# Windowed attention and an MLP mixer on one core: the first pair's tail in one piece, seven-product units in batches 3 and 5, a new order of loads

## Chip, cores and metric

The kernel runs on one core of a Trainium2 chip. The metric is the device time of one execution in microseconds (us). Every number here is from the runs of the kernel before the change or from one profiled execution of it.

## What is computed

Eight batches of 576 positions, eight heads of 64. Attention looks back over a window of 128 positions with a linear bias for each head; its output, eight heads side by side, is the 512-wide input of a mixer with a layer over positions and a layer over channels.

```python
def _attn_ref(q, k, v):                       # each 8 x 8 x 576 x 64
    scores = scale * np.matmul(q, k.transpose(0, 1, 3, 2))
    bias = slopes[:, None, None] * (-np.abs(rel))[None, :, :]
    mask = (rel >= 0) & (rel < 128)
    scores = np.where(mask, scores + bias[None], -1e9)
    attn = np.exp(scores - np.max(scores, axis=-1, keepdims=True))
    attn = attn / (np.sum(attn, axis=-1, keepdims=True) + 1e-09)
    return np.matmul(attn, v)

def _moe_ref(x, w_tok1, w_tok2, w_ch1, w_ch2):  # x: 8 x 576 x 512
    xt = x.transpose(0, 2, 1)
    h = np.maximum(xt @ w_tok1, 0.0) @ w_tok2    # 576 -> 256 -> 576
    u = x + h.transpose(0, 2, 1)
    h2 = np.maximum(u @ w_ch1, 0.0) @ w_ch2      # 512 -> 1536 -> 512
    return u + h2
```

## The kernel before

**Tiles.** Batches go in pairs. A pair has nine blocks of 128 rows: blocks 0 to 3 are the first 512 positions of its first batch, 4 to 7 those of its second, and block 8 (`TAIL`) holds the last 64 positions of both, 64 rows each. Inputs are cast to bf16 as they are loaded, by DMAs that POOL issues (line 521). Five buffers hold q and k of a block, five hold v.

**Stages of a batch.** `side(b)` (line 887) is attention and the token layer: for each block its turn (q and k transposed into `qkT`), scores (line 684), exponential on ACT (line 707), mask on DVE (line 717), the product with v (line 750), reciprocal and scaling on DVE (lines 763 and 766). Then `token_mix`: the first token product (lines 795 and 805), its relu (line 813), the second (line 838), the addition that makes `ub` on DVE (line 856), and the turn of `ub` to `uT`, by TensorE for batches 0 and 1 and by DMA from SP after that (line 864). `main(b)` (line 1007) is the channel layer: `chunk(t)` computes one of twelve tiles of the hidden layer with four matmuls of 512 columns (line 1035) and a relu (line 1041); `tail_piece` does the tail (line 1078) in odd batches; then `second(b)` (line 1149) runs the second layer as seven products in place of eight (line 1212), which need sums of hidden tiles made on DVE (line 1060), and evicts them (line 1183). The order of the seven is the list `PRODUCTS`. `side(b + 1)` runs interleaved with `main(b)`.

**Turns.** A block is turned either by eight TensorE transposes (line 644) and a copy out of PSUM (line 650, on DVE or ACT), or by one DMA transpose from SP (line 633). `FROM_QK` is the running number of the first block that goes by DMA; the first pair has numbers 0 to 8.

**The first pair's tail.** Its q, k and v are loaded in two halves, one batch each. The first half is in the list `LOADS` as q8, k8, v8; the second half comes as lq8, lk8, lv8, later in the list, into the same buffer (`rewrites`). Two memsets (lines 542 and 543) clear the buffer's second half first. The block is turned in `side(0)` and again in `side(1)`, when the second half is there (the condition in line 900).

**Seven-product units.** `unit(b, u, ...)` (line 927) computes four hidden tiles at once by the same scheme of seven products in place of eight: 28 matmuls of 256 columns (line 957) for the 16 of 512 columns that four chunks have. Three of the seven products go one after the other over one PSUM bank after a first one, with the bank read in between. It needs four differences of `uT` made on DVE (`halves`, line 921), sums of weights made once (line 600), three copies out of PSUM (line 972), three additions (line 981), three relus in SBUF (line 983) and one relu out of PSUM (line 1001). `UNITS[b]` says how many of the three groups of four tiles of batch b go this way: before, three in batch 7 and none elsewhere. Units are the last groups of their batch.

**Order.** A planner in the kernel file (`Plan.run`, line 127) simulates the engines and puts the instructions of each engine in an order: of what is ready first, by rank. Ranks get random shifts from `SEEDS`, one per batch. `marks["wait"]` (line 1262) lists operations of `main(b)` that come only behind the last scores of `side(b + 1)`: with `UNIT_LATE` the first products of a unit, with `SECOND_LATE` those of the second layer. POOL's order is not planned: it is the order of `LOADS`, then the other pairs' blocks, then late stores. Where TensorE is idle early on, matmuls on zeros are put in (line 1268). `HALF`, `RATES` and the like are the planner's own figures; they only shape the order.

Of the kernel before, what the change touches and what calls it, by code (L numbers as in the profile page):

```python
# [20 lines left out]
class Buf:  # L21
    def __init__(self, ring, choice):
        self.ring, self.choice, self.slot = ring, choice, None
        self.writers, self.parts, self.users, self.later = [], {}, [], []
# [41 lines left out]
class Plan:  # L66
# [9 lines left out]
    def op(self, eng, cost, emit, rank, makes=(), adds=(), rewrites=(), part=None, uses=(), reads=(), needs=(),  # L76
# [4 lines left out]
        o = Op()  # L81
# [14 lines left out]
        for b in many(rewrites):  # L96
            o.deps.update(u for u in b.users if u not in b.later)
            b.later.append(o)
            b.writers.append(o)
            o.bufs.append(b)  # L100
        if part is not None:
            b, key = part
# [14 lines left out]
    def slot(self):  # L117
        self.orders += 1
        return self.orders

    def dma(self, emit, descs, packets, makes=(), rewrites=(), order=None, uses=()):
        o = self.op("POOL", 550 + 0.33 * descs, emit, 0, makes=makes, rewrites=rewrites, uses=uses,
                    order=order or self.slot())
        o.packets = packets
        return o
# [184 lines left out]
    def emit(self, spin):  # L310
# [12 lines left out]
        for _, _, go in sorted(work, key=lambda w: w[:2]):  # L323
# [8 lines left out]
FROM_QK = 10  # L332
# [8 lines left out]
PRODUCTS = [1, 5, 6, 2, 3, 7, 4]  # L341
# [5 lines left out]
SEEDS = [63488, 544433, 0, 603260, 673561, 0, 172207, 0, 0]  # L347
SHIFT = 1500.0
UNIT_LATE = True
SECOND_LATE = False  # L350
BIASED = [0, 1, 2]
THIRD = [(4, 5)]
TURNED = False
# [4 lines left out]
UNITS = [0, 0, 0, 0, 0, 0, 0, 3]  # L358
# [7 lines left out]
HALF = 0.7  # L366
# [3 lines left out]
LOADS = ("q2 k1 q1 v1 k2 k3 v0 q3 v2 v8 W1 q8 k8 v3 W2 k6 k5 q5 k4 q6 A0 q4 "  # L370
         "v4 lk8 lq8 k7 A1 q7 v5 A2 B0 v6 A3 v7 lv8 B1 B2 T0 P0 B3")
# [3 lines left out]
def kernel(  # L375
# [16 lines left out]
    P = nc.NUM_PARTITIONS  # L392
# [8 lines left out]
    TAIL = 2 * NC  # L401
# [109 lines left out]
    def load(name, pr, blk, parts, order=None):  # L511
        got = block(pr, blk)
        buf = got["v" if name == "v" else "qk"]
        src = {"q": q, "k": k, "v": v}[name]

        def to():
            return buf()[:, :, 0:D] if name == "v" else buf()[:, "qk".index(name), :, :]

        for b, s0, n, p0 in parts:
            def go(b=b, s0=s0, n=n, p0=p0):  # L520
                nc.gpsimd.dma_start(out=to()[p0 : p0 + n, :, :], in_=rows(src, b, s0, n))  # L521
            kw = {"makes": buf} if order is None else {"rewrites": buf, "order": order}
            plan.dma(go, n * H, 1024 if n == P else 520, **kw)
# [20 lines left out]
    lw1, lw2, lw2t, lc1, lc2, later = [], [], [], [], [], []  # L544
# [342 lines left out]
    def side(b, rank):  # L887
# [360 lines left out]
    for name, order in later:  # L1248
        load(name, 0, TAIL, parts_of(0, TAIL)[1:2], order)
# [52 lines left out]
```

## Time and profile before

| | |
|---|---|
| three runs | 280.22 us median (279.9 to 280.82) |
| profiled execution | 280.18 us; span from first to last instruction 278.0 us |
| granted TensorE clock | 1.000 (mean) |
| TensorE matmuls | busy 270.4 us, 97%, of it 8.9 us on zeros, all before 24.8 us |
| VectorE (DVE) | busy 210.0 us, 76% |
| ScalarE (ACT) | 136.2 us, 49% |
| GpSimd (POOL) | 116.3 us, 42%, issuing loads |

The span is 2.2 us shorter than the execution's time. Busy times of TensorE count a matmul to its modelled end, so neighbours overlap: sixteen matmuls of 512 columns show 379 ns each, yet follow each other at 216 ns. A matmul's price is therefore read from the start of one group to the start of the next.

### The profile page before, as it was taken

Reading aid. Unit: us, or ns where it says so; the run is one execution under the profiler, and the core shown is the slowest. Engines: PE = TensorE matmul, PEld = TensorE weight load, DVE = VectorE, ACT = ScalarE, POOL = GpSimd, SP = SyncE. Lnnn points to the kernel's source line nnn. Section 1 sums busy time; section 2 is a strip of 40 time slices with the busy share of each in tenths; the row PEclk is TensorE's granted clock in tenths of the full one; section 3 lists DMA queues with packets and bytes.
Section 4 is the critical chain, followed back from the end, with each engine's and each line's share of the span. In section 5 each row is a group of like instructions: output and inputs, shape, how many; then the busy total and the mean of one; then the engine's idle time right before and its main releaser. Section 6 shows DMA issues by size and latency. Waiting matters only on the chain.

```text
span 278.0 us, 7069 instructions
## 1 busy us (share of the span) xinstructions
PE 270.4 (97%) x2871; PEld 181.7 (65%) x2871; DVE 210.0 (76%) x486; ACT 136.2 (49%) x216; POOL 116.3 (42%) x146
## 2 busy tenths in 40 slices
PE   7989999999999999999999999999999999999994
PEld 4865755676686546595667655586666755489983
DVE  8467799968897569964898469862978569877972
ACT  5563996336970298007860087206951077215500
POOL 8998848940382018900594008800480320022000
PEclk9999999999999999999999999999999999999999
DMA  9999999999599689999999999979799930052014
GB/s 132 151 159 170 191 191 179 156 140 232 73 127 154 137 211 128 132 136 202 174 137 158 201 174 75 146 123 207 136 135 112 171 134 2 8 142 98 2 59 130
DMA packets 167535, 38.43 MB, mean 138 GB/s; under 512 B 155792, under 2 KB 166672, under 8 KB 167504
## 3 DMA queue, kind: packets, MB, share of 16 engines
q0 software_dynamic: 116112, 20.03, 92.5%
q1 hardware_dynamic: 50352, 17.70, 31.6%
q8 instruction: 22, 0.36, 0.5%
q10 hardware_dynamic: 1040, 0.26, 0.4%
q14 instruction: 9, 0.07, 0.1%
HBM read 35.85 MB, written 9.44 MB: 163 GB/s over the span
## 4 chain that ended last, share of the span: by engine, by line
PE 85%; DVE 6%; POOL 4%; DMA 2%; issue 0%; ACT 0%; POOLq 0%
PE ps L1212 25%; PE ps L1035 24%; PE ps L750 6%; PE ps L684 6%; PE ps L838 4%; PE ps L795 4%; PE ps L1078 4%; PE ps L1123 4%; PE ps L957 3%; POOL qk L521 2%; DMA v<-in_v_dram 2%; DVE s L1060 1%; POOL v L521 1%; PE ps L644 1%; DVE WT L582 1%; PE ps L873 1%
## 5 line engine op out<-in xcount | busy, mean ns | idle before, releaser
L1035 PE MATMUL ps<-uT,WC 128*128 128x512 bf16 x328 | 79.5, 379 | 0.0
L1041 ACT ACTIVATE r<-ps 128x512 bf16<-128x512 f32 x75 | 44.3, 602 | 57.4 <-PE ps L1035 52.9
L707 ACT ACTIVATE pe<-ps 128x1024 bf16<-128x1024 f32 (+1 forms) x76 | 63.5, 888 | 18.1 <-PE ps L684 17.7
L521 POOL DMA_DIRECT2D v<-in_v_dram x40 | 34.4, 862 | 89.9 <-PE ps L750 88.2
L1035 PEld LDWEIGHTS <-WC 128*128 128x128 bf16 x328 | 29.1, 98 | 28.3
L717 DVE TENSOR_TENSOR pe<-pe,mask 128x1024 bf16<-128x1024 bf16 (+1 forms) x62 | 37.1, 607 | 8.0 <-ACT pe L707 7.3
L1212 PEld LDWEIGHTS <-r 128*128 128x128 bf16 x384 | 36.9, 98 | 7.9 <-issue 0.7
L521 POOL DMA_DIRECT2D qk<-in_q_dram x39 | 34.0, 877 | 2.8 <-PE ps L750 1.4
L521 POOL DMA_DIRECT2D qk<-in_k_dram x39 | 34.1, 883 | 2.1 <-DMA v<-in_v_dram 1.1
L1212 PEld LDWEIGHTS <-s 128*128 128x128 bf16 x288 | 27.5, 98 | 6.3 <-issue 1.8
L766 DVE TENSOR_TENSOR xb<-ps,rt 128x256 bf16<-128x256 f32 (+1 forms) x73 | 29.5, 419 | 0.8
L750 PEld LDWEIGHTS <-pe 128*128 128x128 bf16 (+1 forms) x560 | 21.6, 100 | 9.6 <-DVE pe L717 2.6
L750 PE MATMUL ps<-v,pe 128*128 128x65 bf16 (+1 forms) x560 | 26.2, 194 | 1.2 <-DMA v<-in_v_dram 1.2
L1212 PE MATMUL ps<-WC,r 128*128 128x256 bf16 x192 | 25.4, 273 | 0.0
L1212 PE MATMUL ps<-WT,s 128*128 128x256 bf16 x192 | 24.2, 273 | 0.0
L1212 PE MATMUL ps<-WT,r 128*128 128x256 bf16 x192 | 23.7, 273 | 0.0
L1183 DVE TENSOR_TENSOR ob<-ps,ub 128x512 f32<-128x512 f32 x22 | 15.2, 689 | 10.1 <-PE ps L1212 10.0
L856 DVE TENSOR_TENSOR ub<-ps,xb 128x512 bf16<-128x512 f32 x34 | 21.4, 684 | 1.4 <-PE ps L838 1.2
L684 PEld LDWEIGHTS <-qkT 64*128 64x128 bf16 x560 | 14.8, 94 | 10.9 <-issue 9.7
L763 DVE RECIPROCAL rt<-ps 128x4 f32<-128x4 f32 (+1 forms) x76 | 12.3, 175 | 10.1 <-PE ps L750 9.4
L684 PE MATMUL ps<-qkT 64*128 64x128 bf16 (+1 forms) x304 | 19.4, 216 | 0.0
L838 PE MATMUL ps<-r,W 128*128 128x512 bf16 x64 | 16.1, 379 | 0.1
(96 smaller groups left out, 336.4 us busy)
## 6 DMA issues: line engine op xcount, KB each, us to landing
out_dram<-ob SPq DMA_DIRECT2D x17, 256.0 KB, 2.5
v<-in_v_dram POOLq DMA_DIRECT2D x32, 128.0 KB, 4.8
qk<-in_q_dram POOLq DMA_DIRECT2D x31, 128.0 KB, 4.9
qk<-in_k_dram POOLq DMA_DIRECT2D x31, 128.0 KB, 4.8
WC<-in_moe_w_ch_dram POOLq DMA_DIRECT2D x8, 384.0 KB, 9.0
out_dram<-raw SPq DMA_DIRECT2D x7, 256.0 KB, 2.6
out_dram<-ob POOLq DMA_DIRECT2D x5, 256.0 KB, 2.9
out_dram<-raw POOLq DMA_DIRECT2D x3, 256.0 KB, 3.0
```

The costliest lines, as they stand in the source:

```text
L521: nc.gpsimd.dma_start(out=to()[p0 : p0 + n, :, :], in_=rows(src, b, s0, n))
L684: pe_.matmul(wide(e)[:, i, kind, a:z], lhsT=ts[kb]()[e * D : (e + 1) * D, NHP + i, :], rhs=ts[blk]()[e * D : (e + 1) * D, i, a:z], start=n ...
L707: act_.activation(out=pb()[:, e, :, lo:, c0:c1_], in_=wide(e)[:, :, lo:, c0:c1_], func=ACT.Exp, scale=scale)
L717: dve_.tensor_tensor(out=o, in0=o, in1=heads(mk, es), op=ALU.mult)
L750: pe_.matmul(view()[a:z, at, i, :], lhsT=pb()[:, e, i, kind, a:z], rhs=vb()[:, h, 0 : D + 1], start=m == 0, stop=m == len(mms) - 1, skip_g ...
L766: dve_.tensor_tensor(out=x4(), in0=view()[r0:r1_, :, :, 0:D], in1=rt()[r0:r1_, 0:n, :, :].broadcast_to([r1_ - r0, n, 4, D]), op=ALU.mult)
L838: pe_.matmul(ht()[:, hs], lhsT=W2[:, j, c * P : (c + 1) * P], rhs=r1()[:, j, :], start=j == 0, stop=j == NJ - 1 and not fold)
L856: plan.op("DVE", 690, lambda blk=blk, ht=ht, hs=hs: dve_.tensor_tensor(out=ub()[:, blk, :], in0=ht()[:, hs], in1=xb()[:, blk, :], op=ALU.a ...
L1035: pe_.matmul(ct()[:, :], lhsT=WC1[:, cb, t * P : (t + 1) * P], rhs=uT()[:, cb, :], start=cb == 0, stop=cb == NCB - 1)
L1041: plan.op("ACT", 600, lambda t=t, ct=ct: act_.activation(out=r2()[:, t, :], in_=ct()[:, :], func=ACT.Relu), rk, part=(r2, t), uses=[ct], o ...
L1183: dve_.tensor_tensor(out=v, in0=bk().rearrange("p (c n) -> p c n", c=2), in1=src, op=ALU.add)
L1212: pe_.matmul(bk()[:, c * HN : (c + 1) * HN], lhsT=l(t, c), rhs=w(t), start=first, stop=g == 1 and t == HK - 1, skip_group_check=True)
```

## The change

The first pair's tail is loaded with both halves at its place in `LOADS` (still two DMAs for each of q, k and v), the memsets and the machinery for a later rewrite go, and it is turned once. `FROM_QK` goes from 10 to 9, so the first block of the second pair is turned by DMA. `UNITS` gives batches 3 and 5 one unit each. `SECOND_LATE` and `TURNED` are switched on: the second layer's opening products come behind the next side's last scores, and the bias matmuls of the first blocks (line 693) behind that block's turn. `PRODUCTS`, `SEEDS`, `LOADS` and `HALF` get other values.

```diff
 class Buf:
-        self.writers, self.parts, self.users, self.later = [], {}, [], []
+        self.writers, self.parts, self.users = [], {}, []
...
-    def op(self, eng, cost, emit, rank, makes=(), adds=(), rewrites=(), part=None, uses=(), reads=(), needs=(),
+    def op(self, eng, cost, emit, rank, makes=(), adds=(), part=None, uses=(), reads=(), needs=(),
            after=0.0, order=None, bus=0.0, other=None, mode=0, behind=()):
...
-        for b in many(rewrites):
-            o.deps.update(u for u in b.users if u not in b.later)
-            b.later.append(o)
-            b.writers.append(o)
-            o.bufs.append(b)
...
-    def slot(self):
+    def dma(self, emit, descs, packets, makes=(), uses=()):
         self.orders += 1
-        return self.orders
-
-    def dma(self, emit, descs, packets, makes=(), rewrites=(), order=None, uses=()):
-        o = self.op("POOL", 550 + 0.33 * descs, emit, 0, makes=makes, rewrites=rewrites, uses=uses,
-                    order=order or self.slot())
+        o = self.op("POOL", 550 + 0.33 * descs, emit, 0, makes=makes, uses=uses, order=self.orders)
...
-FROM_QK = 10
+FROM_QK = 9
...
-PRODUCTS = [1, 5, 6, 2, 3, 7, 4]
+PRODUCTS = [1, 5, 6, 2, 7, 3, 4]
...
-SEEDS = [63488, 544433, 0, 603260, 673561, 0, 172207, 0, 0]
+SEEDS = [299663, 80952, 553840, 849187, 0, 759155, 0, 0, 0, 0]
...
-SECOND_LATE = False
+SECOND_LATE = True
...
-TURNED = False
+TURNED = True
...
-UNITS = [0, 0, 0, 0, 0, 0, 0, 3]
+UNITS = [0, 0, 0, 1, 0, 1, 0, 3]
...
-HALF = 0.7
+HALF = 0.9
...
-LOADS = ("q2 k1 q1 v1 k2 k3 v0 q3 v2 v8 W1 q8 k8 v3 W2 k6 k5 q5 k4 q6 A0 q4 "
-         "v4 lk8 lq8 k7 A1 q7 v5 A2 B0 v6 A3 v7 lv8 B1 B2 T0 P0 B3")
+LOADS = ("k1 q1 k2 q3 k3 q2 v0 v3 W1 v1 q8 v2 k8 q5 v8 W2 k4 k5 k6 q4 A0 v5 "
+         "q6 q7 A1 v4 v6 k7 A2 A3 B0 v7 B1 B2 P0 T0 B3")
...
-    def load(name, pr, blk, parts, order=None):
+    def load(name, pr, blk, parts):
...
-            kw = {"makes": buf} if order is None else {"rewrites": buf, "order": order}
-            plan.dma(go, n * H, 1024 if n == P else 520, **kw)
+            plan.dma(go, n * H, 1024 if n == P else 520, makes=buf)
...
-    last = block(0, TAIL)
-    plan.op("DVE", 180, lambda b=last["qk"]: dve_.memset(b()[R:P, :, :, :], 0.0), -90, makes=last["qk"])
-    plan.op("DVE", 180, lambda b=last["v"]: dve_.memset(b()[R:P, :, 0:D], 0.0), -90, makes=last["v"])
...
-            load(what, 0, n, parts_of(0, n)[0:1])
-        elif what in ("lq", "lk", "lv"):
-            later.append((what[1], plan.slot()))
+            load(what, 0, n, parts_of(0, n))
...
-                    if (pr, w) not in qkT or (u == TAIL and pr == 0):
+                    if (pr, w) not in qkT:
                         transposes(pr, w, rank(0 if by_transfer(pr, w) else 450))
...
-    for name, order in later:
-        load(name, 0, TAIL, parts_of(0, TAIL)[1:2], order)
```

In `LOADS`, W1 and W2 are the token layer's weights, A0 to A3 quarters of the first channel layer's, B0 to B3 of the second's, P0 and T0 the small pieces of the token weights for the tail. W1 is two DMAs. Block 0's q and k come ahead of the list from SP and ACT (line 484).

More of the change, by code (lines that the diff above doesn't have):

```diff
@@ L346 @@
 SUMS_AT = 60e3
-SEEDS = [63488, 544433, 0, 603260, 673561, 0, 172207, 0, 0]
+SEEDS = [299663, 80952, 553840, 849187, 0, 759155, 0, 0, 0]
 SHIFT = 1500.0
 UNIT_LATE = True
-SECOND_LATE = False
+SECOND_LATE = True
 BIASED = [0, 1, 2]
 THIRD = [(4, 5)]
-TURNED = False
+TURNED = True
 SLANT = 4.0e3
@@ L540 @@
             plan.op("DVE", 190, lambda i=i: dve_.memset(W1p[(1 - i) * R : (2 - i) * R, i, :], 0.0), -90)
-    last = block(0, TAIL)
-    plan.op("DVE", 180, lambda b=last["qk"]: dve_.memset(b()[R:P, :, :, :], 0.0), -90, makes=last["qk"])
-    plan.op("DVE", 180, lambda b=last["v"]: dve_.memset(b()[R:P, :, 0:D], 0.0), -90, makes=last["v"])
-    lw1, lw2, lw2t, lc1, lc2, later = [], [], [], [], [], []
+    lw1, lw2, lw2t, lc1, lc2 = [], [], [], [], []
     for item in LOADS.split():
```

## Prediction

> **What bounds the kernel.** First the busy shares, then the 40 slices, then busy time by stage, last the chain.
>
> ```profile
> span 278.0 us, 7069 instructions
> PE 270.4 (97%) x2871; PEld 181.7 (65%) x2871; DVE 210.0 (76%) x486; ACT 136.2 (49%) x216; POOL 116.3 (42%) x146
> PE   7989999999999999999999999999999999999994
> ```
>
> TensorE (PE) is busy from the fourth slice on. Matmul ends are modelled, so I count idle time and pace instead: waits for other engines put down to PE total 3.2 us, of it 3.0 before 19 us (1.2 at the start, 0.6 on block 0's casts, 1.2 on v), and fillers on zeros end at 24.8 us. Before that point the loads decide, behind it whatever TensorE has to do.
>
> ```profile
> 18.81 0.40 PE L750 MATMUL ps<-v,pe 128*128 128x65 bf16 x8 [1.18 <-DMA v<-in_v_dram]
> 19.67 0.20 PE L684 MATMUL ps<-qkT 64*128 64x64 bf16 x2
> ...
> 23.37 0.59 PE L805 MATMUL ps<-xb,W1p 64*128 64x512 bf16 x2
> ...
> 24.63 1.03 PE L838 MATMUL ps<-r,W 128*128 128x512 bf16 x4
> ```
>
> In these lines of the timeline block 3's v lands at 18.8, the tail's scores follow at 19.7, and the last token product (L805) waits for the tail; L838 at 24.6 opens the dense part. Next, who has room there (busy us of PE, PEld, DVE, ACT, POOL in each stretch):
>
> ```profile
> 30.00:44.00 14.00, 14.00 (x196) 8.66 (x194) 12.74 (x39) 13.25 (x21) 9.60 (x13) 1.00 1.55 193
> 44.00:58.00 14.00, 13.83 (x117) 8.59 (x114) 13.63 (x28) 6.51 (x14) 11.86 (x16) 1.00 2.19 155
> 140.00:160.00 20.00, 20.00 (x202) 14.23 (x196) 14.56 (x30) 4.10 (x7) 8.99 (x11) 1.00 1.73 169
> 200.00:210.00 10.00, 10.00 (x141) 6.53 (x136) 7.80 (x22) 6.75 (x10) 7.50 (x9) 1.00 1.87 135
> ```
>
> From 30 to 58 DVE is nearly full as well, and ACT to 44; around 140 and 200, where batches 3 and 5 end their first layer, DVE has a quarter free. The chain agrees:
>
> ```profile
> PE 85%; DVE 6%; POOL 4%; DMA 2%; issue 0%; ACT 0%; POOLq 0%
> ```
>
> **Step 1, the tail turned once.** Eight transposes and a copy go. From the start at 33.85 to the next group's start at 34.30 eight cost 0.45 us. The copy was ACT's, 1.05 at 35.41, in the stretch where ACT is 13.25 of 14.00 busy. Credit 0.45; bounds 0, if DVE's full stretch behind it sets the pace anyway, and 0.45, since TensorE saves no more. The memsets at 4.4 (0.48 and 0.27) open block 0's casts; block 1 waits for its loads behind them, so no credit.
>
> **Step 2, block 0 of the second pair by DMA.** Eight transposes at 56.03 go (next start 56.48: 0.45), with ACT's 1.01 copy at 56.7, which nobody waited for. The DMA transpose is new on SP: q and k land at 48.2 and 49.1, SP's first transpose was issued at 51.64, so SP is free. One took 3.1 to 9.0 us to land (median 3.9), so at worst 58; the block's scores run at 67.0. It also holds up the loads behind it by 2 to 4 us (a v load beside one took 7.6 where its neighbours took 6.1); the nearest user, block 1's scores at 69.2, had its turn landed at 59.7. Hidden, 9 us of cover. Credit 0.45.
>
> **Step 3, two units.** Four chunks cost 4 x 0.865 = 3.46 on the chain; batch 7's rows show 28 matmuls in 3.06. Credit 2 x 0.40 = 0.80. What it adds per unit: on DVE four differences of 0.42, three additions of 0.69, three relus of 0.29, together 4.6; on ACT three copies of 0.59 and a relu of 0.60 against four relus of 0.60, equal. The differences fit where `uT` has landed (124.7, 186) and DVE is idle (4.0 of 10 busy from 120). The weight sums (L600) are made at 62 to 66 already. The other 2.95 us fall behind the next side's last scores (140, 203), where DVE still has norms, sums and the token relu to do, and `ub`, then SP's turns, wait behind them. Cover: in batch 3 the last `uT` piece landed at 156.1 and L1035 started at 159.3, 3.2 us to spare; in batch 5, 219.0 and 220.6, 1.6 us. So batch 3 is hidden, batch 5 may lose up to 2.95 - 1.6 = 1.35. I take 0.2, since DVE has 2.2 of those ten us free; the bounds are 0 and 1.35.
>
> **Step 4, the new order of loads.** Total bytes stay. Block 2's and 3's q and k come sooner; v's last (block 2) is the 14th DMA where block 3's was the 15th. But the tail now has six DMAs ahead of W2, not three, with q5 among them: k8 complete is 16th, before 14th. POOL's ends of issue: eight loads by 8.7, W1 1.28, v1 0.87, two halves 1.38, v2 0.87, two halves 1.38: 14.5. Behind an issue's end q8, k8 and v3 landed after 4.1, 3.9 and 5.0 us, so k8 lands at 18.4 to 19.5; I take 18.5, its own row, since v3's late landing came right behind W1's 256 KB, which now lie further ahead. From k8's landing (16.85) eight transposes ended 0.45 later, and a DVE copy takes 0.69: scores 1.25 after landing, at 19.7 to 20.75, before 19.67. I take +0.1 (bounds -0.3, if PE, no longer held by v, has the tail's way clear, and +1.3, with v8's second half, issued to 16.7, also late). W2 ends its issue at 17.5, lands by 23.8 (its neighbours took 5.5 to 6.3): L838 needs it at 24.6, 0.8 of cover. Next A0: five items later, 21.8 + 6.6 = 28.4 where it landed at 26.2; L1020 used it at 28.57. Block 6's q comes behind A0 and v5, near 30; its transposes ran at 27.5. So 25 to 30 us is thinner by one block's transposes (0.45) and perhaps the first chunk: take 0.2, bounds 0 and 1.0. From B1 on the list has moved the same bytes as before.
>
> A rule against this step: the Trainium skill, "DMA: Bandwidth & Descriptors" (Rules for kernel authors), advises one transfer on 128 partitions in place of two on halves, and calls what is under 64 KB mostly overhead. The halves are 64 KB; q8 and k8 landed 0.46 us apart, whole loads 0.85, so here a half costs a half. If by the rule each cost a whole one, as an estimate, the two more ahead of k8's end would add 0.8, and the sum would be -0.4 in place of -1.2.
>
> **Step 5, orders.** `SECOND_LATE` delays opening products (L1212 at 46.9, 77.7, 110.2, 145.3, 171.7, 203.5): all but those at 171.7 and 203.5 ran behind the last scores already, or within a us. They are fillers; another takes the place. `PRODUCTS` puts product 3 (1.31 us) between 7 and 4, which share a bank whose eviction takes 0.69: cover, worth 0 to 0.3 at the end, taken as 0. New seeds reshuffle ranks: 0, bounds -0.5 and +0.5.
>
> **Sum.** -0.45 - 0.45 - 0.80 + 0.2 + 0.1 + 0.2 = -1.2 us. Against the profiled execution, 280.18 (span 278.0 and 2.2 around it, 0.04 under the median): **279.0**. Its own range is 277.7 to 280.2.
>
> **Rivals.**
> *Nothing gained (280.3).* The side's DVE work sets the pace: tail credit lost (0), block credit 0.45 and batch 3's 0.40 kept, batch 5 loses 1.35 - 0.40, the loads 0.1: 280.3. For: DVE 13.63 of 14.00. Against: PE waits 0.2 there.
> *The loads (280.8).* k8 and v8 at their late bound +1.3, the thin stretch +1.0: -1.7 + 2.3 = +0.6. For: the chain is POOL and DMA until 18.8. Against: fillers show room, and v no longer holds block 3.
> *Slower, by the units (282.5).* In batch 7 the first product of a unit starts at 248.8 and the last relu ends at 256.1, 7.3 us for 3.06 of its own products, because one bank is filled, read, filled. Batch 7 fills the gaps with other units. A lone unit behind the last scores has values, token products and tail pieces. If 2 us of the 4.2 stay open in each, 280.18 - 1.7 + 4.0 = 282.5; it decides from 0.85 a unit on. Against: 14 us of second layer stand between, though half of it needs the unit's tiles.
> Beside it the Trainium skill, "TensorEngine Tiling (Array Packing)" (PSUM Bottleneck), says that speeding up TensorE leaves the reading of PSUM as it was, which can then bound. That is this rival; batch 7's dense rows don't show it.
> *Not done as said:* L957 would not count 140, L1035 296, L644 72.
>
> **Chances.** Forecast 0.55, nothing gained 0.14, loads 0.10, units 0.19, not as said 0.02. About 0.3%, 0.84 us, is what a measurement can tell here: under 279.4 is most of the forecast case and nothing else, with some luck of the seeds: 0.57. Over 281.1 is the units and the loads' end: 0.22. Between: 0.21. The range is 277.5 (credits 1.7, loads -0.3, seeds -0.5, so 277.7, and 0.2 for the end) to 282.2, leaving out the units' worst.
>
> **What would show it.** L838 first at 24.3 to 25.0, no filler behind it; L644 x72, the last near 35; PE without waits at 140 to 148 and 203 to 210; L1035 of batches 4 and 6 about 1.2 and 1.5 us earlier than 159.3 and 220.6, less the early loss. Wrong, if PE waits on DVE L981 or ACT L972, if L838 comes after 26, or if the dense part has gaps at 25 to 30 over a us.

## The result, and the profile after

| | time, median | range |
|---|---|---|
| before (ten runs beside it) | 280.37 us | 279.9 to 280.85 |
| after (ten runs) | 281.52 us | 280.85 to 282.78 |

The ratio is 1.0054, interval 1.0033 to 1.0075: 0.5% slower, where 0.4% faster was forecast. In a second series of runs the changed kernel came out the same: 281.69 (ratio 1.0064, 1.0031 to 1.0096). The profiled execution after took 282.7 with a span of 280.8, at the upper end of its runs, so the two spans stand 2.7 us apart where the medians stand 1.2 to 1.7 apart. (In the diff shown above the new `SEEDS` have one zero too many at the end; the list has nine entries.)

First the head of the page and TensorE's line of the 40 slices, after:

```profile
span 280.8 us, 7138 instructions
...
PE 270.4 (96%) x2888; PEld 183.6 (65%) x2888; DVE 217.6 (78%) x504; ACT 135.7 (48%) x226; POOL 115.6 (41%) x146
...
PE   6999999999999999997999999998999999999994
```

TensorE's busy time is the same 270.4 as before, though the change took work from it. Two slices in the middle, at 127 and 191 us, are no longer full. The groups by line tell what the equal sum is made of. Before, then after (columns: busy us and mean ns of one behind the first bar, idle time and its releaser behind the second):

```profile
L1035 PE MATMUL ps<-uT,WC 128*128 128x512 bf16 x328 | 79.5, 379 | 0.0
L1268 PE MATMUL ps<-zero 128*128 128x128 bf16 (+1 forms) x73 | 8.9, 266 | 1.2 <-DVE zero L485 1.2
L644 PE MATMUL ps<-ident,qk 128*128 128x128 bf16 x88 | 6.9, 220 | 0.6 <-DVE qk L536 0.6
```

```profile
L1020 PE MATMUL ps<-uT,WC 128*128 128x512 bf16 x296 | 71.2, 379 | 2.5 <-DMA uT<-ub 2.5
L1251 PE MATMUL ps<-zero 128*128 128x128 bf16 (+1 forms) x82 | 10.7, 273 | 1.2 <-DVE zero L476 1.2
L629 PE MATMUL ps<-ident,qk 128*128 128x128 bf16 x72 | 5.7, 220 | 1.2 <-DVE qk L526 1.2
```

Counted to the end of each matmul or the start of the next, whichever is first, TensorE's balance is: chunks 73.2 to 66.4, unit products 9.2 to 15.3, so -0.7; transposes of q and k 5.3 to 4.2, -1.1; fillers 7.3 to 9.5, +2.2; gaps over 0.06 us 2.3 to 5.1, +2.8; all else -0.5. The work fell by about what was forecast. The idle time, of which fillers are a part, grew by 5.0.

The early half of it is in the timeline of TensorE. After, the lines that answer to those of before:

```profile
16.16 0.65 PE L735 MATMUL ps<-v,pe 128*128 128x65 bf16 x16 [0.63 <-DMA v<-in_v_dram]
...
20.58 0.20 PE L669 MATMUL ps<-qkT 64*128 64x64 bf16 x2
...
24.23 0.59 PE L790 MATMUL ps<-xb,W1p 64*128 64x512 bf16 x2
...
25.39 0.81 PE L823 MATMUL ps<-r,W 128*128 128x512 bf16 x3
```

TensorE waits for v of block 1 (landed at 16.12), which lies behind the 256 KB of W1 in the new list. The tail's scores come at 20.58 (before 19.67), the first second-token product at 25.39 (24.63), batch 1's at 50.63 (49.36). The late half is in the timeline at the two thin slices:

```profile
124.28 1.07 PE L1063 MATMUL ps<-uTt,WC 128*128 128x128 bf16 x16
125.18 1.47 PE L1197 MATMUL ps<-WT,r 128*128 128x256 bf16 x12
126.49 1.06 PE L1063 MATMUL ps<-uTt,WC 128*128 128x128 bf16 x16
129.05 1.02 PE L1020 MATMUL ps<-uT,WC 128*128 128x512 bf16 x4 [1.50 <-DMA uT<-ub]
```

```profile
189.56 1.06 PE L1063 MATMUL ps<-uTt,WC 128*128 128x128 bf16 x16
191.56 1.04 PE L1020 MATMUL ps<-uT,WC 128*128 128x512 bf16 x4 [0.95 <-DMA uT<-ub]
```

Before, the same place in batch 3 has no wait:

```profile
124.40 1.47 PE L1212 MATMUL ps<-WT,r 128*128 128x256 bf16 x12
125.71 1.89 PE L1035 MATMUL ps<-uT,WC 128*128 128x512 bf16 x8
```

At the start of the first layer of batches 3 and 5 TensorE has done all the second-layer work and tail pieces that its order puts there, and waits for the last piece of `uT`. Both kernels issue batch 3's five turns (four of `uT`, and the tail's as the third) in the same order, but before, the last piece landed at 124.73 and its first user started at 125.71. Now batch 3's second token product starts at 117.72 (115.84 before) and the last piece lands at 128.92. Of these 4.2 us about half is a later issue (124.52, before 122.38) and half a slower landing (4.40 us after issue, before 2.36). In batch 5 the order differs: before, the tail's turn was the last of the five; now it goes ahead of the last piece of `uT`, which lands at 191.52.

The busy times of the stretches shown before, and the shares of the chain that ended last:

```profile
30.00:44.00 14.00, 13.43 (x196) 8.24 (x194) 11.69 (x33) 12.23 (x18) 8.06 (x11) 1.00 1.57 192
44.00:58.00 14.00, 13.95 (x129) 8.96 (x126) 13.78 (x33) 5.75 (x13) 10.89 (x14) 1.00 2.20 159
140.00:160.00 20.00, 20.00 (x209) 14.95 (x207) 17.82 (x38) 8.30 (x18) 10.81 (x13) 1.00 1.86 133
200.00:210.00 10.00, 10.00 (x168) 8.10 (x166) 9.60 (x26) 8.03 (x15) 8.87 (x11) 1.00 1.58 110
```

```profile
PE 72%; DVE 10%; DMA 9%; POOL 5%; issue 1%; SPq 1%; ACT 0%; POOLq 0%; DVEq 0%
```

From 30 to 44 TensorE has gaps now (0.57 at 34.3, for a v). Around 140 and 200, where the units' extra DVE work falls, DVE is nearly full (17.82 of 20, 9.60 of 10), yet TensorE has no gap there. The chain has 9% DMA where it had 2%.

### The profile page after: what moved, and what is told of

It is laid out like the page before. It is cut to its first block, busy times and chain, and to the rows that moved or that the text cites. A ratio compares the mean times of both kernels' runs of the same rounds, so it can differ in the third digit from the quotient of the medians.

```text
span 280.8 us, 7138 instructions
## 1 busy us (share of the span) xinstructions
PE 270.4 (96%) x2888; PEld 183.6 (65%) x2888; DVE 217.6 (78%) x504; ACT 135.7 (48%) x226; POOL 115.6 (41%) x146
## 4 chain that ended last, share of the span: by engine, by line
PE 72%; DVE 10%; DMA 9%; POOL 5%; issue 1%; SPq 1%; ACT 0%; POOLq 0%; DVEq 0%
PE ps L1197 23%; PE ps L1020 19%; PE ps L942 6%; DMA v<-in_v_dram 5%; PE ps L735 5%; PE ps L669 5%; PE ps L780 4%; PE ps L1108 4%; PE ps L823 3%; POOL qk L512 3%; DMA uT<-ub 3%; PE ps L1063 3%; DVE pe L702 2%; DVE xb L751 2%; DVE ub L841 1%
## 5 line engine op out<-in xcount | busy, mean ns | idle before, releaser
L1020 PE MATMUL ps<-uT,WC 128*128 128x512 bf16 x296 | 71.2, 379 | 2.5 <-DMA uT<-ub 2.5
L1026 ACT ACTIVATE r<-ps 128x512 bf16<-128x512 f32 x66 | 39.3, 600 | 44.1 <-PE ps L1020 38.5
L1020 PEld LDWEIGHTS <-WC 128*128 128x128 bf16 x296 | 26.2, 97 | 29.3 <-issue 1.8
L751 DVE TENSOR_TENSOR xb<-ps,rt 128x256 bf16<-128x256 f32 (+1 forms) x69 | 28.0, 419 | 0.7
L1197 PE MATMUL ps<-WT,s 128*128 128x256 bf16 x192 | 24.3, 273 | 0.0
L1180 POOL DMA_DIRECT2D out_dram<-ob x5 | 3.6, 725 | 35.9 <-DVE ob L1168 35.9
L1068 ACT ACTIVATE r2t<-ps 128x512 bf16<-128x512 f32 x12 | 7.2, 600 | 23.2 <-PE ps L1063 23.2
```

What stands on the lines that cost most here:

```text
L751: dve_.tensor_tensor(out=x4(), in0=view()[r0:r1_, :, :, 0:D], in1=rt()[r0:r1_, 0:n, :, :].broadcast_to([r1_ - r0, n, 4, D]), op=ALU.mult)
L1020: pe_.matmul(ct()[:, :], lhsT=WC1[:, cb, t * P : (t + 1) * P], rhs=uT()[:, cb, :], start=cb == 0, stop=cb == NCB - 1)
L1026: plan.op("ACT", 600, lambda t=t, ct=ct: act_.activation(out=r2()[:, t, :], in_=ct()[:, :], func=ACT.Relu), rk, part=(r2, t), uses=[ct], o ...
L1197: pe_.matmul(bk()[:, c * HN : (c + 1) * HN], lhsT=l(t, c), rhs=w(t), start=first, stop=g == 1 and t == HK - 1, skip_group_check=True)
```

## The experiments

All times of this section are medians with the ratio to the kernel before on the same chip, the interval in brackets. "First" and "second landmark" are the starts of the second token product of batch 0 and of batch 1 in the profiled execution (24.63 and 49.36 before, 25.39 and 50.63 after).

### The changed kernel again, and three single undoings

**a_again**, no edit.

> The changed kernel once more, unedited. In its first profile (282.7 us, the slow end of 280.9 to 282.8) TensorE waited 1.5 and 0.95 us for the last piece of uT of batches 3 and 5, while a pause of all DMA packets of 1 to 2 us lay on that piece. Theory A (the waits for uT make the spread and a good part of the loss): a profile of a run near 281.0 has under 1 us of such waits, one near 282.7 has 2 us and more. Rival B (the loss is all in the first 50 us, from the loads): the waits are the same 2.5 us whatever the time, and the first token product of batch 1 (L823, second group) is over 1 us later than the 49.4 of before in both.

281.69, 1.0064 [1.0031, 1.0096]. The profiled execution took 283.31, longer than the first one's 282.7, and its waits on `uT` are shorter (1.0 and 0.8), so they don't make the spread: theory A misses. The landmarks, 25.93 and 51.92, are over a us late, as rival B said. Between them is a new wait, in the thin stretch behind the loads:

```profile
35.31 1.04 PE L1020 MATMUL ps<-uT,WC 128*128 128x512 bf16 x4 [1.45 <-DMA WC<-in_moe_w_ch_dram]
```

**a_nounits**, the units of batches 3 and 5 undone:

```diff
-UNITS = [0, 0, 0, 1, 0, 1, 0, 3]
+UNITS = [0, 0, 0, 0, 0, 0, 0, 3]
```

> The changed kernel with UNITS as before (three in batch 7 alone); the planned order is the same up to batch 3's first layer. Theory A: the units themselves pay: without them the time rises by up to 0.8 us against the changed kernel's median 281.5, to 281.7 to 282.3; the wait for uT of batch 3 near 127 us stays (0 to 1.5), since it lies ahead of any unit. Rival C (the units' work on VectorE and on the PSUM bank costs more than it saves): the time falls by 1 us or more, to 280.5 or less.

283.69, 1.012 [1.0093, 1.0147]: 2.0 us slower than with the units and above theory A's range. Taking the units out does not bring the time back. How much they pay can't be taken from it: the planner ordered everything behind batch 3 anew, and the gaps of TensorE behind 52 us sum to 4.5 us, 1.9 in a_again.

**a_tailturn**, the turn of the tail's `ub` on SP kept behind the four pieces of `uT`:

```diff
-  part=(uTt if blk == TAIL else uT, blk), reads=[(ub, blk)], bus=1000))
+  part=(uTt if blk == TAIL else uT, blk), reads=[(ub, blk)], bus=1000,
+  behind=turned.get(b, [])[:] if blk == TAIL else []))
```

> The changed kernel with one wait more in the plan: from batch 3 on the tail's turn (uTt) goes to SP's queue only behind the four main blocks' turns; SP then sends four uT and one uTt in every odd batch. Theory A: the last uT piece of batches 3 and 5 lands 1.3 us sooner, TensorE's waits for it fall under 0.8 us together, and the time falls by 0.5 to 1.5 us, to 280 to 281. Rival B (loads): no more than 0.3 us changes. Rival C (units): no change in kind, the waits were not the cost.

280.45, 1.0012 [0.9983, 1.004], over a wide range (278.79 to 282.32). Its profiled execution took 278.91, 1.5 under the median; in the list of TensorE's waits `uT` doesn't occur:

```profile
PE ps L1252 <- DVE zero L476: 1.2, 1, 1.2
PE ps L629 <- DVE qk L526: 0.3, 1, 0.3
PE ps L629 <- DMA qk<-in_q_dram: 0.3, 1, 0.3
PE ps L669 <- DVE qkT L635: 0.2, 1, 0.2
```

That looked like the late loss explained. Further runs take half of it back. The wait does go with this edit: the four kernels that have it and are planned anew (this one, and a_both, c_v1 and c_w1 below) wait for `uT` 0 to 0.5 us in all, the five without it (after, a_again, a_nounits, and a_taillast and p_v1 below) 1.6 to 3.0. The time does not: the other three with the edit came out at 282.6 to 283.4. And since the planner's order differs from batch 3 on, the turn was not the only thing that moved.

**b_loads**, the kernel before with the loads of the change alone (tail whole and turned once, new `LOADS`, `HALF`, and `TURNED`), and its own seeds:

> Before, with the first part of the change alone: the first pair's tail whole and turned once, the new LOADS, HALF and TURNED; units, FROM_QK, SECOND_LATE, PRODUCTS and SEEDS as before. The 0.45 us of transposes saved are in it. Rival B (loads lose more than a us by 50 us): 281.0 to 282, with the first L823 at 25.2 or later and batch 1's over 1 us later than before's 49.4. If the loads cost what was forecast (0.3): 280.0 to 280.4. Theory A with the early loss as in the profile (0.8 by 25 us, 1.7 by 50): 280.8 to 281.6.

303.01, 1.0817, far above what was expected. With the seeds of the other list the plan falls apart: one wait of 8.2 us for `uT` at 174, fillers up to 59 us. It tells nothing of the loads, but that seeds belong to the settings they were found with.

### The loads, alone and left out

**b_loads2**, as b_loads, with the seeds of the first two parts that came with the new list:

```diff
-SEEDS = [63488, 544433, 0, 603260, 673561, 0, 172207, 0, 0]
+SEEDS = [299663, 80952, 0, 603260, 673561, 0, 172207, 0, 0]
```

> The change of the loads alone (tail whole and turned once, new list, HALF), with the seeds of parts 0 and 1 that were found with it and all other settings and seeds of before. Its order of the first 46 us is that of the changed kernel. Theory 1: first second-token product at 25.2 to 25.5 and batch 1's at 50.4 to 51 (before 24.63 and 49.36). If the early loss were chance of one execution: 24.6 to 25.0 and 49.4 to 49.8. The end: 280.9 to 282 by theory 1 if nothing happens later; the seeds of later parts belong to other loads, so that a wait on uT may put more on top, which would show as gaps of TensorE behind 60 us.

281.69, 1.0084 [1.0059, 1.0109]: the loads, with `TURNED` and the order of the first two parts that came with them, cost 2.0 us. Landmarks 25.11 and 50.23; gaps behind 52 us sum to 0.6. Of the 1.5 us between the two profiled spans 0.9 lie ahead of the second landmark.

**b_rest**, the reverse: the kernel before with everything but the loads and `TURNED`, seeds of its own for the first two parts.

> The kernel before with every setting of the change but the loads: units in batches 3 and 5, block 0 of the second pair turned by DMA, SECOND_LATE, PRODUCTS and the new seeds of parts 2 to 8; list of loads, halved tail and the seeds of parts 0 and 1 as before. Theory 1 (the loads lose some 0.8 us by the first second-token product and up to 1.5 by batch 1's): L838 first at 24.6 as before, batch 1's near 49.4, and the time lies 0.8 to 1.5 below the changed kernel's, 279.8 to 280.8, with the waits on uT still there if these come from the units and the seeds. Theory 2 (all of the loss is in the middle, the order of SP's turns and of the sides): 281 to 282, no better than the changed kernel. If the loads were the only loss, 278.5 to 279.2.

288.36, 1.0301 [1.0243, 1.0358]. Behind 78 us its plan waits in six places (for masks 1.85 and 1.14, for `uT` 0.93), so its time says nothing. Its first 46 us, though, are in the order of the kernel before, and show what the profile of before had hidden:

```profile
17.34 0.40 PE L750 MATMUL ps<-v,pe 128*128 128x65 bf16 x8
...
22.04 0.59 PE L805 MATMUL ps<-xb,W1p 64*128 64x512 bf16 x2
23.30 1.03 PE L838 MATMUL ps<-r,W 128*128 128x512 bf16 x4
```

Here v of block 3 lands at 17.30, where it took until 18.77 in the profiled execution of before, and the first landmark is at 23.30 in place of 24.63.

**b_units**, the kernel before with the units alone (and `SECOND_LATE`).

> The kernel before with the two units alone (and SECOND_LATE, without which no order with them is found). Theory (units pay 1 to 2 us where the order round them leaves no wait on uT): 278 to 279.3. Rival (they pay only against the changed kernel's order, whose chunks ran into late uT): 279.8 to 281.

286.02, 1.0222 [1.0195, 1.0248]: again a plan with waits behind 115 us (`uT` 1.55 and 0.62, second layer 2.2 in four places, a unit of batch 7 1.44). Its landmarks, in the old order, are 23.63 and 48.81.

Taken together, these executions give the landmarks as a sample. Old list and old order of the first parts (before, b_rest, b_units, and s_best below): first 24.63, 23.30, 23.63, 24.82, mean 24.10; second 49.36, 48.30, 48.81, 49.78, mean 49.06. New list and the order that came with it (after, a_again, a_nounits, a_tailturn, b_loads2, a_taillast, a_both, p_turn): first 24.87 to 26.15, mean 25.55; second 49.46 to 51.92, mean 50.80. The new list is 1.45 us behind at the first landmark and 1.74 at the second, with the tail's eight transposes already saved. It is not work moved ahead: but for those transposes TensorE has run as many matmuls of each shape by a landmark in every one of the twelve (five records are missing in s_best). The sample does not part the list from the order of the engines' work and from `TURNED`, which always go with it. Three more executions have other orders: s_old (below), old list, 26.01 and 50.77; b_loads and s_cover (below), new list, 26.27 and 54.41, 25.36 and 51.73. The second landmarks of the last two have more work of the second layer ahead of them (18 and 12 products).

### The place of the tail's scores

**a_taillast**, in `side(3)` the tail's scores pinned behind the fourth full block's, and **a_both**, the same with the edit of a_tailturn:

```diff
-  pb = scores(pr, u, hf, rank(450), wides if b == 1 else ())
+  pb = scores(pr, u, hf, rank(450), (wides if b == 1 else []) +
+              ([marks["score"]] if u == TAIL and b == 3 else []))
```

> The changed kernel with one order pinned: in the side work of batch 3 the tail's scores come behind the four full blocks', as they ran in the kernel before. Theory A (the tail run early puts a full block last, so that batch 3's token products come 2 to 3 us later while TensorE spends its second-layer work, and uT comes too late for batch 3): batch 3's first-layer wait of 1.5 us at 127 goes, its first token product is 2 us closer to 111.4, and the time falls by 0.5 to 1.2, to 280.4 to 281.0. Theory B (the place of the tail makes no odds, only the fifth turn among uT's pieces does): the wait stays, 281.3 to 281.9.

> The changed kernel with both repairs: the tail's scores last in batch 3's side, and the tail's turn behind the four uT pieces on SP. If the two repairs take away different waits: 279.5 to 280.2. If they are two ways to the same end (uT in time for batches 3 and 5): as with the turn alone, 280.2 to 280.7.

284.74, 1.0179 [1.0141, 1.0217], and 282.6, 1.011 [1.0085, 1.0136]. The theory falls: with the tail last, batch 3's first token product starts at 113.96 in place of 114.25, no 2 us sooner, the wait on `uT` in batch 3 stays (0.97), and new gaps come at 110, 117 and 163. In a_both no wait on `uT` is left, but the new gaps are there as well. That the tail ran second was not what made batch 3 late.

### The order of the first loads

In the trace's rows of DMA issues there is a rule that the prediction had not used, though the planner's code has it (its `lanes`): no load is issued by POOL before the load eight places ahead of it has landed. POOL's loads signal eight semaphores in turn (104 to 111 in the trace), and each waits for the one that it is to signal. POOL's timeline, after:

```profile
14.71 0.89 POOL L512 DMA_DIRECT2D qk<-in_q_dram  x1 [0.34 <-issue]
16.03 1.35 POOL L512 DMA_DIRECT2D v<-in_v_dram  x2 [0.43 <-DMA W1p<-in_moe_w_tok_dram]
```

q5 is the 17th load and W1, the 9th, landed at 14.15; v8 is the 18th and W1's second part, the 10th, landed at 15.74. In a_again the pair is 15.34 behind 14.78, in a_taillast 16.18 behind 15.62: always 0.56. Every load behind it moves along.

**c_v1** and **c_w1**, on the kernel of a_tailturn:

```diff
-LOADS = ("k1 q1 k2 q3 k3 q2 v0 v3 W1 v1 q8 v2 k8 q5 v8 W2 k4 ...
+LOADS = ("k1 q1 k2 q3 k3 q2 v0 v3 v1 W1 q8 v2 k8 q5 v8 W2 k4 ...   (c_v1)
+LOADS = ("k1 q1 k2 q3 k3 q2 v0 v3 v1 q8 v2 k8 W1 q5 v8 W2 k4 ...   (c_w1)
```

> The changed kernel with the tail's turn behind the four uT pieces, and in the list of loads v of block 1 one place sooner, ahead of the token weights W1 (256 KB) in place of behind them. Theory (the early loss hangs on v of block 1: in five executions the first second-token product came 9.25 to 9.7 us behind its landing, which lay at 15.4 to 16.7 behind W1): v1 lands at 13 to 13.5, the wait of TensorE for it at 15.5 goes, q5 and v's tail, which were issued 0.3 to 0.6 behind the landing of the load eight places ahead (W1, its second half, v1), no longer wait; the tail's k at 18.3 to 18.7 sets the next bound, its scores at 19.6 to 20.0, the first second-token product at 24.1 to 24.6, and the time 0.4 to 1.0 under 280.4. Rival (k8 and the tail's load in two halves set the early stage): first second-token product stays at 25.0 to 25.5.

> As the one with v1 sooner, but W1 and its small second part stand behind the tail's q and k as well. Theory: the tail's k lands some 2 us sooner, near 16.5, its scores run at 17.6 to 18.2, W1 lands at 18 to 19, in time for the token product; the first second-token product at 22.8 to 23.8, where kernels with the old list had 24.63 and 23.30, and the time 1 to 2 under 280.4. Rival (the order of the loads is not what sets the early stage): first second-token product at 24.6 or later. The planner's order behind it changes too, so the time itself may move by 1 to 2 us either way at 60 to 200 us, which would show as waits of TensorE there.

283.38, 1.0151 [1.0103, 1.0198], and 283.06, 1.0115 [1.0083, 1.0148]. v of block 1 lands at 13.9 in both, as expected, but the first landmark is 25.69 and 24.44: the planner ordered the first 25 us anew and put other work into the room. Both have a wait of 1.15 us for masks at 96. Both also have the tail's turn moved, so that alone doesn't repair the kernel.

Then the order was held fixed: the plan of the changed kernel is made as it is, and single instructions are moved in it.

**p_v1** moves v of block 1 ahead of W1 on POOL, **p_turn** the tail's turn behind the four pieces of `uT` on SP, **p_both** does both.

```diff
     plan.run()
+    plan.ops[at["v1"]].t0 = plan.ops[at["W1"]].t0 - 0.01                 (p_v1, p_both)
+    for b in range(FROM_U, B):                                           (p_turn, p_both)
+        if b % 2:
+            turned[b][-1].t0 = max(o.t0 for o in turned[b]) + 0.01
```

> The changed kernel with its planned order kept on every engine but POOL, where v of block 1 is loaded ahead of W1's two parts in place of behind them. Theory (TensorE waits for v of block 1, 0.63 and 1.06 in two executions, and everything up to the first second-token product is chained to it): the wait at 15.5 goes, the first second-token product at 24.3 to 24.8 where it was 25.39 and 25.93, the time 0.5 to 1.0 lower, 280.6 to 281.2. Rival (the tail's k, at 18.3 to 19.3, holds the first product as well): first second-token product within 0.2 of 25.4, time 281.3 to 281.9.

281.94, 1.0079 [1.0055, 1.0103]: no gain. The wait for v is gone and the tail's scores run 0.9 us sooner, but the time is given back five us later:

```profile
15.37 0.65 PE L737 MATMUL ps<-v,pe 128*128 128x65 bf16 x16
...
19.67 0.20 PE L671 MATMUL ps<-qkT 64*128 64x64 bf16 x2
...
25.55 0.40 PE L631 MATMUL ps<-ident,qk 128*128 128x128 bf16 x4 [1.14 <-DMA qk<-in_k_dram]
25.78 1.03 PE L825 MATMUL ps<-r,W 128*128 128x512 bf16 x4
```

A block's k landed late in this execution (25.50), and its transposes stand ahead of the token product in TensorE's order. So v of block 1 was the first wait of several. That k is a matter of the execution: in p_both, with the same loads and the same order of TensorE to this point, it landed at 23.82 and the first landmark is 24.48.

> The changed kernel with its planned order kept on every engine but SP, where in batches 3 and 5 the turn of the tail's ub is issued behind the four uT pieces in place of ahead of the last two and the last one. Theory (uT's last piece late, by one place in SP's queue): the waits on uT at 127.6 (1.50) and 190.6 (0.95) fall by about 1 us each, to 0.5 and 0 to 0.3, and the time by 1.0 to 2.0, to 279.6 to 280.7. Rival (the gain of the kernel with the turn moved by the planner came from its other order, not from the turn): 281.3 to 281.9, no change.

> Both single moves of the two runs beside it. If the two losses are separate and both theories hold: 279.0 to 280.0, the level of the kernel before or under it. If the early gain is eaten by a later wait: as with the turn alone.

283.04, 1.0109 [1.0074, 1.0144], and 282.24, 1.0102 [1.0065, 1.0138]. In both, and in p_w1nf, the first of batch 3's tail pieces works on the tail of an earlier batch, since in the kept order it runs before the tail's turn. So their results are not those of the changed kernel, and only their times are used. The wait doesn't go; it changes hands (p_turn):

```profile
125.41 1.47 PE L1197 MATMUL ps<-WT,r 128*128 128x256 bf16 x12
128.49 1.05 PE L1063 MATMUL ps<-uTt,WC 128*128 128x128 bf16 x16 [1.61 <-DMA uTt<-ub]
129.38 1.03 PE L1020 MATMUL ps<-uT,WC 128*128 128x512 bf16 x4
```

The chunks start at 129.38 as they did at 129.05. The last piece of `uT` now lands at 125.97, 3 us sooner, but in the kept order a tail piece stands ahead of the chunks, and it waits for the tail's turn (landed 128.45). TensorE needs all five turns at that point, so a move in SP's queue alone does not help; the kernels without the wait have TensorE's order changed as well.

**p_w1nf**, as p_both, with W1 behind the tail's k and the fillers between 15 and 22 us left out:

```diff
+    for i in range(2):
+        plan.ops[at["W1"] + i].t0 = plan.ops[at["q5"] - 1].t0 + 0.01 * (i + 1)
...
-            if a < FILL and z - a > (250 if a > DENSE else 100):
+            if a < FILL and not 15e3 < a < 22e3 and z - a > (250 if a > DENSE else 100):
```

> As with both moves, but W1's two parts are loaded behind the tail's k, and the fillers on zeros between 15 and 22 us are left out (they compute nothing). Theory (with W1 out of the way the tail's k lands near 16.5 and the rest is the chain's own work, of which some 2 us were fillers): scores of the tail at 18 to 19, first second-token product at 23.2 to 24.2, and the time 0.5 to 1.5 under the kernel with both moves, 278 to 279.3. Rival (the token products then wait for W1, or the clock falls without the fillers): first second-token product no earlier than with both moves, or a granted clock under 1.00 before 30 us.

280.56, 1.0034 [1.0017, 1.005]: 1.7 us under p_both. Landmarks 24.38 and 50.09, only 0.1 and 0.4 sooner than in p_both (24.48 and 50.47). The tail's k lands at 16.64, but its scores run at 19.44 behind three waits of 0.5 us for DVE. The gain lies further on: TensorE waits 1.1 us for the tail's turn, in one place, where p_both waits 3.4 in two. The granted clock stays 1.00 without those fillers.

### Seeds found for each setting

**s_old** is the kernel before with everything but the loads and `TURNED`, **s_cover** the changed kernel with the planner told that turns land later. Both have seeds looked for until the planner's own estimate of the end was as low as it could be brought.

```diff
-SEEDS = [63488, 544433, 0, 603260, 673561, 0, 172207, 0, 0]
+SEEDS = [800802, 751850, 665837, 223453, 231983, 0, 0, 860424, 200811]      (s_old)
...
-TURN = [(792.0, 1267.0), (1380.0, 2400.0)]
+TURN = [(792.0, 2700.0), (1380.0, 2800.0)]                                  (s_cover)
-SEEDS = [299663, 80952, 553840, 849187, 0, 759155, 0, 0, 0]
+SEEDS = [3981, 576130, 143578, 17368, 0, 0, 0, 0, 710613]
```

> The kernel before with every setting of the change but the loads (old list, tail loaded in halves and turned twice), as in the run that came out 8 us slow, but with seeds looked for anew until the planner's own estimate of the end was as low as for the two kernels. Theory (the loads cost the changed kernel some 1.6 us by the first second-token product; units and the block by DMA gain 1.0 to 1.3 where nothing waits on uT): first second-token product at 23.3 to 24.7, time 278.3 to 279.4 without waits on uT, up to 280.5 with some. Rival (the loss lies in the units and the orders, not in the loads): 281 or more with the early stage as in the kernel before.

> The changed kernel, loads and all, with the planner told that a turn lands 1.4 us (for uT) and 0.4 us (for q and k) later than it assumed, and seeds looked for anew. Theory (the waits on uT in batches 3 and 5 are lost cover, since the planner's turns land sooner than the chip's): no wait on uT over 0.4 us, first second-token product at 25 to 26 as with these loads, time 279.6 to 280.8. Rival (the cover is paid for elsewhere, or the wait moves to the scores or the masks): 281 to 282 with other gaps of TensorE behind 60 us.

s_old: 279.95, 1.0007 [0.9988, 1.0025]. s_cover: 281.01, 1.0051 [1.0029, 1.0072]. They ran side by side, and differ by the loads, `TURNED`, the planner's cover and the seeds: 1.1 us. In s_cover the wait on `uT` is down to 0.2, and the kernel is as slow as the changed one: its landmarks are 25.36 and 51.73. In s_old no wait on a DMA is left, and it is no faster than the kernel before. The stretch from the second landmark to the end is 227.6 us in s_old, 227.4 in s_cover and 227.3 in a_tailturn, against 228.7 before, each in one execution: the 1.1 to 1.3 that Steps 2 and 3 promised. In s_old and a_tailturn it is not work moved ahead of the landmark: TensorE has run as many matmuls of each shape by then as in before, the tail's transposes and four records that s_old's trace lacks aside. In s_cover it is: twelve products of the second layer more have run by then, 1.3 us at 0.109 each. But s_old's start was late: second landmark 50.77. In that execution the granted clock was low from 8 to 12 us (last section) and the tail's k landed at 18.33, where the other four executions with this list have 16.36 to 16.85. What the seeds did to the start is not told apart from that.

**s_best** should put the two good halves together: everything but the loads and `TURNED`, the old seeds for the first two parts, `TURN = [(792.0, 2200.0), (1380.0, 2800.0)]`, seeds looked for in the other parts.

> The kernel before with every setting of the change but the loads, its own seeds kept for the first two parts, so that the order of the first 46 us is that of the kernel before, the planner told that turns land later (0.9 us for uT, 0.4 for q and k), and seeds looked for anew for the other parts. Theory (the early stage as in the kernel before, first second-token product at 23.3 to 24.7 and batch 1's at 48.3 to 49.4; behind it units and the block by DMA gain 1.0 to 1.3 as in three plans without waits on uT): 278.2 to 279.0 where the kernel before has 279.6, a ratio of 0.995 to 0.998. Rival (the gain behind 50 us is only what plans lose before it): 279.4 to 280.2, ratio 1.000 or more.

280.23, 1.0003 [0.9989, 1.0018]. The early order held (24.82 and 49.78), but the rest took 229.3, with a wait that the planner had not seen, in the side work of batch 2, for banks that ACT's exponentials free:

```profile
81.03 0.19 PE L684 MATMUL ps<-qkT 64*128 64x64 bf16 x1 [0.71 <-ACT pe L707]
81.94 0.19 PE L684 MATMUL ps<-qkT 64*128 64x64 bf16 x1 [0.73 <-ACT pe L707]
```

Without the loads the change is worth nothing that can be measured, in two plans. No version tried beats the kernel before.

## Why the prediction was wrong

**Steps 4 and 5 failed, and each would have turned the sign.** Between the two profiled spans -1.2 was forecast and +2.7 measured. Ahead of the second landmark +1.27 came for -0.15, which is Step 4's failure with Step 1's credit in it; behind it +1.47 for the -1.05 of Steps 2 and 3, and that miss of 2.5 is as large as TensorE's gaps there (2.5, before 0.1), which Step 5 had put at 0.

**Step 4** gave the loads +0.1 at the first landmark and +0.2 behind it, against -0.45 for the tail: a gain of 0.15 by 50 us. The sample says a loss of 1.7, and b_loads2 2.0 at the end. Three things were off. The base: k8 came at 17.8 to 19.3, as worked out, but the step compared it with an execution in which v of block 3 was 0.7 to 1.5 us later than in the three others with the old list and order (18.77; 17.30, 17.77, 18.07). The step put that late landing down to W1; q8 and k8 landed in between, at 16.39 and 16.85. The waiter: it followed k8 alone; v of block 1, moved behind W1's 256 KB, landed at 15.4 to 16.9, held TensorE by up to 1.1 us, and the tail's copy then stood behind those values' scaling on DVE: scores 1.9 us after k8, not 1.25. The queue: with two halves more ahead of W2, and W1 9th, POOL waited for W1's landing, and W2 left POOL 0.2 to 1.6 us behind the 17.5 counted, with all that follows it. The 1.45 of a_again at 35 us is A1, issued 0.6 later than in the first execution and landed 2.1 later, so for the most part slow under way. How much of the early loss is the arrival of the loads and how much the order that came with them stays open: p_v1 and p_w1nf took away the wait for v, and their second landmarks are still 50.47 and 50.09, not 49.06. The rival "the loads" had the mechanism; its price, 0.6 net, was too low, since the bound of +1.3 sat on k8 and v8 only.

The Trainium skill, "DMA: Bandwidth & Descriptors" (Rules for kernel authors), advises against two transfers on halves of the partitions. The estimate that the prediction made from it, a half at the price of a whole, is not what the trace shows. In the changed kernel the two halves of k8 landed 0.41 apart and those of v8 0.42, whole loads 0.83 to 0.85. A half took half the time of a whole, as Step 4 had it. It does take a whole one of the eight places that POOL's loads have.

**Steps 1, 2 and 3 were right as work, and the changed kernel's time shows nothing of it.** TensorE's own work fell by 1.7 (-0.7 units, forecast -0.80; -1.1 transposes, forecast -0.90). Only s_old and a_tailturn, without waits on `uT`, have a stretch behind the second landmark that is shorter by about as much as Steps 2 and 3 said (1.1 and 1.3). No stall showed behind the units: no gap at 140 to 148 and 203 to 210, and batches 4 and 6 start their first layer without a wait. The rival "slower, by the units" came near the time by a mechanism that is absent. (The rival "nothing gained" adds up to 280.4 by its own terms, not 280.3; it changes nothing.)

**Step 5 was too narrow.** It took the new orders at 0, bounds of 0.5 each way. Kernels with the same settings but another plan lie at 280.45, 281.01 and 281.6, and those with one or two small edits, planned anew, at 282.6 to 284.7. Waits of 1 us and more come up in most plans, on `uT`, masks or exponentials; the kernel before has 0.1 us of gaps behind 52 us, the least of all the plans here. The changed kernel's waits on `uT` (1.8 to 2.5 in three executions) are such a case. That the order makes `uT` late is an inference from the plans without the wait; which part of the order does it was not found.

What told right: `L629` x72, `L942` x140, `L1020` x296, no filler behind the first second-token product. What told wrong: that product at 25.39, not 24.3 to 25.0, and the first layers of batches 4 and 6 2.1 and 4.2 us later, not 1.2 and 1.5 earlier.

**Open**: why s_old and s_best, with the work saved and the waits of s_old small, are no faster. In s_old four of twelve executions have a mean clock of 0.992 (280.25 to 280.87), the profiled one among them; the other eight average 279.5, still no gain on 279.6. No execution of these eight was profiled. And whether there is an order with both the early half of the kernel before and a rest without waits: only s_best tried for it.

## What to carry to other kernels

At 97% on one engine, work taken away is worth what the rest of the schedule can hand in sooner; ask which arrival ends the next wait, and how much cover it had. A step that moves loads is costed for every load that a wait could fall on, against several executions of the kernel before, since one execution's arrivals scatter by more than the effect; and count places in the issuing queue as well as bytes. Where a planner reorders everything on each edit, undoing one part is no clean experiment: keep the order and move one instruction, or look for new seeds for both sides.

## What the hardware showed

POOL's loads run eight deep in both kernels: none is issued sooner than 0.28 us behind the landing of the load eight places ahead, whatever its size. They signal eight semaphores in turn, so the depth may be the program's; whether the chip would take more, no run shows.

In three executions of the changed kernel's middle order (after, a_again, p_v1) the last `uT` piece of batch 3 took 4.40, 3.93 and 3.94 us to land and that of batch 5 4.21, 4.03 and 3.98, where the two turns just ahead took 2.3 to 2.4. In batch 3 of the first execution all transfers stood still meanwhile. The bytes moved in 40 slices of 0.15 us from 124 to 130, after, with the queue that carries instructions:

```profile
GB/s 0 0 26 230 288 270 60 1 0 0 109 61 251 271 213 21 0 0 0 0 0 2 7 10 10 9 10 9 5 118 198 215 205 208 207 208 164 183 113 205
...
q8 instruction: 1, 0.02, 1.7%
```

From 126.4 to 128.3 next to nothing moves. A load of instructions of 16 KB began at 125.6. The kernel before has such a pause at 127.1 to 128.2, behind an instruction load at 126.4, but its last piece had landed by 124.73. In p_turn the last `uT` piece landed at 125.97, in 2.3 us, just as the instruction load began. That the instruction load causes the pause was not tried.

In s_old's profiled execution the granted clock fell to 0.60 between 8 and 12 us:

```profile
8.00:12.00 4.00, 4.00 (x44) 3.11 (x42) 0.69 (x1) 1.17 (x3) 4.00 (x6) 0.60 2.25 143
```

From 8 to 11 us it was 0.50. TensorE was busy 2.52 of the 4 us ahead of that, hardly less than in the changed kernel (2.66), whose clock stayed at 1.00. What decides it the runs don't show.
